# Constants carried by the first key row, an earlier row sum, and gate weights in three blocks, in a two-layer decode kernel

## The chip, the cores and the metric

The kernel runs on one core of one Trainium2 chip. The metric is the device time of one execution in microseconds (us). Repeated runs of one kernel agree within about 0.3%, which is 1.5 us here.

## The reference

One token goes through two identical layers. A layer is attention over the last 4,096 cached positions of 32 heads (head size 192), then a gated MLP; both have a layer norm and a residual.

```python
D, H, DH, F, W = 640, 32, 192, 1536, 4096          # from the inputs' shapes
def attn(x, k_cache, v_cache, wq, wo):
    q = (x @ wq).reshape(heads)                     # 1 x 32 x 192
    p = softmax(einsum("qd,kd->qk", q, k[-W:]) * DH**-0.5)
    return (p @ v[-W:]).reshape(1, H * DH) @ wo
def mlp(x, w_gate, w_up, w_down):
    return (sigmoid(x @ w_gate) * (x @ w_up)) @ w_down
for layer in range(2):                              # the same weights and cache in both
    x = x + attn(layernorm(x), ...)
    x = x + mlp(layernorm(x), ...)
```

Keys and values are 201 MB in bf16 if they are read for both layers. Nothing is reused within a layer: this is a kernel that streams.

## The kernel before

Heads are handled in 16 pairs. A pair's query weights and keys ("a", 28,416 B per partition) and its values and output weights ("b", the same size) fill two of seven slots in the large buffer `big`; the MLP weights use a region behind the slots. A list `seq` fixes the order of all loads, and each load is issued by the sync engine (SP) as soon as the products that still read its destination are done. Three pairs, and the keys of a fourth, are kept for layer 2.

```python
    cst = sb("cst", [P, CE + CE % 2], BF16)       # selectors, masks and x: 241 columns
    big = sb("big", [P, NSLOT * UNIT + ME], BF16, 256)
    # ... cut ...
    MD = {"wg0": (0, 0, 6), "wg2": (6, 6, 12), ...}          # gate weights in two loads of six blocks
    MAFTER = {"d0": ("wg0",), "d1": ("wg1",), "u2": ("wg2",), "u3": ("wg3",), ...}  # who frees whose place
    # ... cut ...
    pg.dma(q_dma(cst[:, 0:CE], cx), "x", wr=[res("cst")], q="adma")   # on the scalar engine's queue
    while seq_pos[0] < 2:                         # first key row, then the first pair load
        assert try_load(seq[seq_pos[0]])
        seq_pos[0] += 1
    # ... cut ...
        def step(p, prev):                        # one pair of layer 1
            ... ; Q(p, 0); QK(p, 0); soft(0, ...); expo(); PVmm(prev, prev % 2); ET(p % 2); PVt(prev % 2)
    # ... cut: the end of the first attention layer ...
            p = NPAIR - 1
            PVmm(p, 1)            # value product of the last pair, waits for its load
            RS(1, 2)              # row sum: ones x (sums of the exponentials), fp32
            PVn(p - 1, 0)         # output product of the pair before
            PVt(1, False)         # transposes of the last pair's result
            PVn(p, 1)             # its output product; then residual, norm, MLP
```

## Time and profile before

| | before |
|---|---|
| time, median of the first 3 runs | 513.43 us |
| span of the profiled run | 511.9 us |
| bytes moved, mean rate | 218.47 MB, 427 GB/s |
| share of the span: TensorE / VectorE / ScalarE busy | 51% / 20% / 17% |
| the last large load lands, the last of two small ones behind it, then the end | 508.97, 509.82, 511.9 us |

From the page of the kernel before: the DMA engines' share in 40 slices (9 is 90% or more), the packets, two queues, the chain that ended last, and the group of the query product (busy time and mean of one, then the idle time before it and who ended most of that).

```profile
DMA  9999999999999999999999999999999999999997
DMA packets 9670, 218.47 MB, mean 427 GB/s; under 512 B 1201, under 2 KB 1586, under 8 KB 4658
q1 hardware_dynamic: 9506, 218.14, 99.3%
q10 hardware_dynamic: 144, 0.06, 0.0%
DMA 64%; PE 22%; DVE 8%; ACT 3%; issue 2%; SPq 1%; DVEq 0%; POOL 0%; ACTq 0%; POOLq 0%
L414 PE MATMUL bank<-sh,big 128*128 128x1 bf16 x465 | 17.1, 166 | 133.2 <-DMA big<-in_uc_dram 130.7
```

The engines that move data are busy in every slice and those that compute are not; the query product spends 130.7 us waiting for loads. Queue q10 is the constants' own: 128 rows and 16 completion packets.

From the timeline of the kernel before, the start (start, length, engine, line, operation, and in brackets the idle time before it with what ended it):

```profile
0.78 0.37 ACTq L217 DMA_DIRECT2D cst<-in_cx_dram  x1
15.41 0.17 DVE L364 TENSOR_SCALAR sc<-cst 128x2 f32<-128x2 bf16 x1 [13.29 <-DMA cst<-in_cx_dram]
...
25.37 0.22 DVE L469 TENSOR_SCALAR sc<-sc 128x2 f32<-128x2 f32 x1
...
28.02 0.56 PE L414 MATMUL bank<-sh,big 128*128 128x1 bf16 x15 [2.83 <-DMA big<-in_uc_dram]
```

The first pair's chain starts when the constants come, at 15.41, ends at 25.6, and TensorE then waits for the next load until 28.02.

And the end of the first attention layer:

```profile
270.59 0.81 PE L494 MATMUL o<-big,et_sb 128*2 128x384 bf16 x8 [0.69 <-DMA big<-in_uc_dram]
271.32 0.59 PE L475 MATMUL bank<-sc 128*128 128x2 f32 x2
...
271.82 0.54 PE L529 MATMUL bank<-sh,big 128*128 128x1 bf16 x15
...
272.45 0.30 PE L515 MATMUL bank<-cst,o_sb 128*128 128x1 bf16 x6
...
275.16 0.96 PE L684 MATMUL scores<-sh,big 128*128 128x1 bf16 x30 [0.60 <-DVE sc L380]
275.75 0.80 SPq L217 DMA_DIRECT2D big<-in_wd_dram  x2
```

Row sum, another pair's output product and only then the transposes stand between the last value product and the MLP; the first down-weight loads are issued at 275.75, when the products of the first three gate blocks are done.

### The profile page before, as it was taken

The page shows a single profiled execution, that of the slowest core. Times are in us where ns is not written, and L with a number is a line of the kernel's source. Part 1 is how long each engine was busy: PE and PEld are TensorE (multiplying, and loading weights), DVE is VectorE, ACT ScalarE, POOL GpSimd, SP SyncE. Part 2 cuts the span into 40 slices and gives each one's busy share as a digit, 9 for nine tenths or more (in the row PEclk, how much of TensorE's full clock was granted, in tenths as well). Part 3 has the DMA queues.
Part 4 walks back from the last instruction along what each step waited for, and adds up shares of the span by engine and source line. Part 5 has one row for each costly group of instructions (what it writes and reads, how often), then busy time and mean ns, then how long its engine had stood idle before and what let it go on. Part 6 is the DMA issues. An engine that isn't in the chain of part 4 may idle for free.

```text
span 511.9 us, 8586 instructions
## 1 busy us (share of the span) xinstructions
PE 260.5 (51%) x3716; PEld 137.7 (27%) x3716; DVE 102.1 (20%) x386; ACT 85.5 (17%) x173; POOL 4.2 (1%) x31
## 2 busy tenths in 40 slices
PE   0463455345533364436566767775725345533666
PEld 0221222122212131223234434432312122212335
DVE  0221221112210221012121333231201112210312
ACT  1110111011101111011121023221211011101221
POOL 0010000000000000000000000000000000000000
PEclk9999765655766755666575568675665655766755
DMA  9999999999999999999999999999999999999997
GB/s 422 435 423 426 419 431 424 431 435 431 453 431 431 436 435 426 431 435 426 424 416 421 414 441 431 434 430 434 439 435 444 435 431 422 436 431 417 429 428 296
DMA packets 9670, 218.47 MB, mean 427 GB/s; under 512 B 1201, under 2 KB 1586, under 8 KB 4658
## 3 DMA queue, kind: packets, MB, share of 16 engines
q1 hardware_dynamic: 9506, 218.14, 99.3%
q8 instruction: 13, 0.21, 0.1%
q10 hardware_dynamic: 144, 0.06, 0.0%
q14 instruction: 7, 0.06, 0.0%
HBM read 218.20 MB, written 0.00 MB: 426 GB/s over the span
## 4 chain that ended last, share of the span: by engine, by line
DMA 64%; PE 22%; DVE 8%; ACT 3%; issue 2%; SPq 1%; DVEq 0%; POOL 0%; ACTq 0%; POOLq 0%
DMA big<-in_uc_dram 54%; PE scores L432 8%; DMA big<-in_wd_dram 6%; PE o L494 6%; DMA big<-in_wu_dram 4%; DVE sc L442 3%; PE bank L448 2%; ACT e_sb L458 2%; PE bank L414 2%; PE bank L529 1%; PE bank L464 1%; ACT diag L445 1%; SPq L217 1%; DVE sc L477 1%; DVE qs L420 1%
## 5 line engine op out<-in xcount | busy, mean ns | idle before, releaser
L432 PE MATMUL scores<-big,qs 128*32 128x512 bf16 x744 | 81.2, 602 | 10.3 <-DVE qs L420 9.5
L414 PE MATMUL bank<-sh,big 128*128 128x1 bf16 x465 | 17.1, 166 | 133.2 <-DMA big<-in_uc_dram 130.7
L494 PE MATMUL o<-big,et_sb 128*2 128x384 bf16 x1024 | 75.1, 460 | 8.0 <-DMA big<-in_uc_dram 3.8
L445 ACT ACTIVATE diag<-cst,sc 128x128 f32<-128x128 bf16 x32 | 12.8, 401 | 306.1 <-DVE sc L442 298.0
L442 DVE TENSOR_REDUCE sc<-scores 128x1 f32<-128x1024 f32 x31 | 37.9, 1224 | 76.9 <-PE scores L432 76.9
L414 PEld LDWEIGHTS bank<-sh,big 128*128 128x128 bf16 x465 | 14.7, 103 | 136.3 <-DMA big<-in_uc_dram 113.6
L448 PE MATMUL bank<-diag,sc 128*128 128x128 f32 x64 | 22.7, 452 | 46.4 <-ACT diag L445 46.4
L458 ACT ACTIVATE e_sb<-scores,sc 128x1024 bf16<-128x1024 f32 x31 | 37.3, 1205 | 42.2 <-DVE sc L453 39.9
L420 DVE TENSOR_TENSOR qs<-bank,cst 128x96 bf16<-128x96 f32 x30 | 7.7, 258 | 161.9 <-PE bank L414 161.9
L494 PEld LDWEIGHTS o<-big,et_sb 128*2 128x2 bf16 x1024 | 27.5, 106 | 43.2 <-issue 28.2
L432 PEld LDWEIGHTS scores<-big,qs 128*32 128x32 bf16 x744 | 23.9, 130 | 42.9 <-issue 29.7
L448 PEld LDWEIGHTS bank<-diag,sc 128*128 128x128 f32 x64 | 14.2, 277 | 72.2 <-ACT diag L445 69.8
L501 ACT CAST o_sb<-o 128x384 bf16<-128x384 f32 x64 | 29.6, 475 | 21.5 <-PE o L494 21.3
L529 PE MATMUL bank<-sh,big 128*128 128x1 bf16 x480 | 17.1, 165 | 15.0 <-DVE sh L518 15.0
L468 DVE CAST et_sb<-bank 128x64 bf16<-128x64 f32 x32 | 7.2, 225 | 70.0 <-PE bank L464 70.0
L529 PEld LDWEIGHTS bank<-sh,big 128*128 128x128 bf16 x480 | 14.5, 99 | 17.5 <-DVE sh L518 12.3
L449 DVE TENSOR_REDUCE sc<-bank 128x2 f32<-128x128 f32 x32 | 9.3, 292 | 43.6 <-PE bank L448 43.6
L464 PE MATMUL bank<-cst,e_sb 128*128 128x8 bf16 x256 | 11.7, 169 | 8.0 <-ACT e_sb L458 7.9
L464 PEld LDWEIGHTS bank<-cst,e_sb 128*128 128x128 bf16 x256 | 8.9, 101 | 23.7 <-issue 17.1
L475 PE MATMUL o<-sc 128*128 128x2 f32 x62 | 14.0, 295 | 0.6 <-ACT o_sb L501 0.6
L475 PEld LDWEIGHTS o<-sc 128*128 128x128 f32 x62 | 12.1, 243 | 2.1 <-ACT o_sb L501 1.3
L477 DVE RECIPROCAL sc<-o 64x1 f32<-64x1 f32 x62 | 10.2, 164 | 9.3 <-PE o L475 7.6
(81 smaller groups left out, 111.0 us busy)
## 6 DMA issues: line engine op xcount, KB each, us to landing
big<-in_uc_dram SPq DMA_DIRECT2D x20, 7104.0 KB, 22.7
big<-in_uc_dram SPq DMA_DIRECT2D x11, 3552.0 KB, 20.5
big<-in_uc_dram SPq DMA_DIRECT2D x2, 3072.0 KB, 18.0
big<-in_uc_dram SPq DMA_DIRECT2D x8, 480.0 KB, 6.5
big<-in_uc_dram SPq DMA_DIRECT2D x1, 2784.0 KB, 13.3
big<-in_uc_dram SPq DMA_DIRECT2D x1, 2304.0 KB, 10.5
big<-in_uc_dram SPq DMA_DIRECT2D x1, 2048.0 KB, 11.0
big<-in_wg_dram SPq DMA_DIRECT2D x2, 960.0 KB, 16.0
```

The lines of the kernel that those rows point to most:

```text
L414: ins = t.matmul(qe[:, i:i + 1], lhsT=w[:, c * 2 * DH + c0:c * 2 * DH + c0 + P], rhs=xq[:, c:c + 1], start=(c == 0), stop=(c == DC - 1))
L432: ins = t.matmul(sc_x[1 + b][32 * j:32 * j + 32, :], lhsT=qs[:, y, k, :], rhs=slot(sa, WQE + k * W + (4 * b + j) * 512, 512), start=(k == ...
L442: pg.op("dve", lambda v: v.reduce_max(out=mx, in_=sc_x[0][:], axis=AX.X), wr=[res("mx")], ex=sc_x[3:5])
L445: pg.op("act", lambda a: a.mul(out=diag[:], in_=ident, mul=mx), rd=[res("cst"), res("mx")], wr=[res("diag")])
L448: pg.op("pe", lambda t: t.matmul(dmx[:, 0:P], lhsT=ones_f, rhs=diag[:], start=True, stop=True), rd=[res("diag"), res("ones")], ex=[rb[2]])
L458: pg.op("act", lambda a: a.activation(out=e_sb[:], in_=sc_x[0][:], func=ACT.Exp, bias=nbias, scale=srs_c, accum_out=rowsum), rd=[res("nbia ...
L464: ins = t.matmul(qe[:, 0:2 * NB].rearrange("p (r x) -> p r x", r=2)[:, :, 4 * b:4 * b + 4], lhsT=e_sb[:, b * P:(b + 1) * P], rhs=sel, star ...
L475: pg.op("pe", lambda t: t.matmul(sm, lhsT=ones_f, rhs=rs2[z], start=True, stop=True), rd=[res(f"rs2{z}"), res("ones")], wr=[res("rsum")], ...
L477: rb[bk].last["dve"] = pg.op("dve", lambda v, h=h: v.reciprocal(out=Rn[z][64 * h:64 * h + 64], in_=sm[64 * h:64 * h + 64, h:h + 1]), rd=[r ...
L494: ins = t.matmul(o8[h][32 * j:32 * j + 2, 0:2 * DH].rearrange("p (a d) -> p a d", a=2), lhsT=et_sb[:, z, h * NB + 2 * u:h * NB + 2 * u + 2 ...
L501: pg.op("act", lambda a, h=h: a.copy(out=o8_sb[:, :, h * DH:(h + 1) * DH], in_=o8[h][:, 0:2 * DH].rearrange("p (a d) -> p a d", a=2)), wr= ...
L529: ins = t.matmul(yT[:, j:j + 1], lhsT=wo[:, c * D + j * P:c * D + (j + 1) * P], rhs=oTb[z][:, c:c + 1], start=False, stop=(c == 2), skip_g ...
```

## The change

The intent: one small, inefficient load less and an earlier first step; a shorter chain from the last values to the MLP; and a first gate block that doesn't wait for six. The constants are placed behind the first key row, in a gap between the fifth and the sixth slot, and arrive with that row.

```diff
-    cst = sb("cst", [P, CE + CE % 2], BF16)
-    big = sb("big", [P, NSLOT * UNIT + ME], BF16, 256)
-    M0 = NSLOT * UNIT
+    GAP = -(-CE // P) * P
+    big = sb("big", [P, NSLOT * UNIT + GAP + ME], BF16, 256)
+    M0 = NSLOT * UNIT + GAP
+    cst = big[:, 5 * UNIT:5 * UNIT + GAP]
-    MD = {"wg0": (0, 0, 6), "wg2": (6, 6, 12), **...}
+    MD = {"wg0": (0, 0, 3), "wg1": (3, 3, 9), "wg3": (9, 9, 12), **...}
     def slot(s, o, n):
-        return big[:, PLACE[s] * UNIT + o:PLACE[s] * UNIT + o + n]
+        o += PLACE[s] * UNIT + (GAP if PLACE[s] > 4 else 0)
+        return big[:, o:o + n]
+            ext = CE if it[1:] == (0, 0) else 0          # the first key row alone
-            pg.dma(q_dma(slot(s, o0, UNIT - o0), a_in(it[2], o0)), ...)
+            pg.dma(q_dma(slot(s, o0, UNIT + ext - o0), a_in(it[2], o0, UNIT + ext)), ...)
-    pg.dma(q_dma(cst[:, 0:CE], cx), "x", wr=[res("cst")], q="adma")
             p = NPAIR - 1
+            RS(1, 2)
             PVmm(p, 1)
-            RS(1, 2)
+            PVt(1, False)
             PVn(p - 1, 0)
-            PVt(1, False)
             PVn(p, 1)
# cut: two asserts, the kernel's argument cx, the empty queue "adma", the host layout
```

More of the change, by code (lines that the diff above doesn't have):

```diff
@@ L109, in decode_kernel @@
 @with_exitstack
-def decode_kernel(ctx: ExitStack, nc, cx: bass.AP, uc: bass.AP,
+def decode_kernel(ctx: ExitStack, nc, uc: bass.AP,
                   wg_d: bass.AP, wu_d: bass.AP, wd_d: bass.AP, wl_d: bass.AP, out: bass.AP):
@@ L186, in decode_kernel @@
           "d0": (0, 0, 3), "d1": (3, 3, 6), "u2": (6, 7, 10), "u3": (9, 10, 12), "d2": (11, 6, 9), "d3": (14, 9, 11), "d4": (16, 11, 12)}
-    MD = {"wg0": (0, 0, 6), "wg2": (6, 6, 12), **{k: v for k, v in MW.items() if k[0] != "w"}}
+    MD = {"wg0": (0, 0, 3), "wg1": (3, 3, 9), "wg3": (9, 9, 12), **{k: v for k, v in MW.items() if k[0] != "w"}}
     MAFTER = {"d0": ("wg0",), "d1": ("wg1",), "u2": ("wg2",), "u3": ("wg3",), "d2": ("wg3", "u0"), "d3": ("u1",), "d4": ("u1",)}
@@ L263, in try_load @@
             first = min(ss, key=PLACE.get)
-            assert abs(PLACE[ss[0]] - PLACE[ss[1]]) == 1 and first == ss[p % 2]
+            assert abs(PLACE[ss[0]] - PLACE[ss[1]]) == 1 and first == ss[p % 2] and PLACE[first] != 4
             pg.dma(q_dma(slot(first, 0, 2 * UNIT), uc[p]), f"c{l}{p % 2}", wr=[rslot[x] for x in ss])
@@ L271, in try_load @@
             o0 = WQE if it[1:] == (1, 3) else 0
-            pg.dma(q_dma(slot(s, o0, UNIT - o0), a_in(it[2], o0)), f"c{it[1]}{it[2] % 2}" if it[1:] in ((0, 15), (1, 4), (1, 5), (1, 6), (1, 13)) else f"a{it[1]}_{it[2]}", wr=[rslot[s]])
+            ext = CE if it[1:] == (0, 0) else 0
+            assert not ext or PLACE[s] == 4
+            pg.dma(q_dma(slot(s, o0, UNIT + ext - o0), a_in(it[2], o0, UNIT + ext)), f"c{it[1]}{it[2] % 2}" if it[1:] in ((0, 15), (1, 4), (1, 5), (1, 6), (1, 13)) else f"a{it[1]}_{it[2]}", wr=[rslot[s]] + ([res("cst")] if ext else []))
         elif k == "b":
@@ L870, in decode_kernel @@
     emit("dma", nc.sync, 1, NFIRST, known_sp)
-    emit("adma", nc.scalar)
     with nc.Block() as block:
@@ L941, in _layout @@
     wl = np.ascontiguousarray(wdn[:, (FC - 2) * D:].reshape(P, 2, 2, D // 2).transpose(0, 2, 1, 3).reshape(P, 2 * D))
-    return dict(cx=cx, uc=uc, wg=blk(wg), wu=blk(wu), wd=wdn, wl=wl)
+    uc[0][:, UNIT:UNIT + CE] = cx
+    return dict(uc=uc, wg=blk(wg), wu=blk(wu), wd=wdn, wl=wl)
 def kernel(**inputs):
```

## The prediction

> **What bounds the kernel now.** The DMA engines, from the first microsecond to the last three. The page gives 218.47 MB at a mean of 427 GB/s and DMA slices of 9 everywhere but the last (7); PE is busy 51%, and idles 133 us in front of the query product, nearly all released by a load. The chain of waits is 64% DMA. The trace's packet records say it more sharply: counting packets open at each moment, all 16 engines are occupied between about 2 and 508 us (under 0.3 us idle per engine there), and the main queue's packets sum to 508.2 us per engine of a span of 511.9. The rest is about 1.0 us before the first packet and 2.9 us after the last load (timeline: it lands at 508.97, then twenty matmuls, copies, the store). So only the engines' work per byte, the start and the tail can move the time.
>
> **What the change removes, adds, moves.**
> 1. Constants. The separate load (60.2 KB, 482 B a row, on the scalar engine's queue) costs 0.224 us per engine (about 27 ns a row). The Trainium skill, "DMA: Bandwidth & Descriptors", "Issuing engines are not separate DMA queues", says that all issuing queues share the 16 engines and interleave; the trace agrees: these packets lie one by one between the main queue's. Rows of 28,416 and 56,832 B take 1,053 and 2,098 ns, 36.8 ns per KB, so 482 B more is an estimated 18 ns, 0.14 us per engine over 8 rows. Saved: 0.08 us.
> 2. Earlier compute. The constants landed near 15.05 us and are first used at 15.41; the first key row's packets were done near 10.2. So the first norm, query, scores and softmax should start near 10.6, almost 5 us earlier. But that chain ends at 25.6 and waits for the second load until 28.0; the wait only grows. On the critical path: 0.
> 3. Gate weights. Two loads of 7,680 B rows become rows of 3,840, 7,680, 3,840 B: by measured packets (291 and 149 ns, 9 ns for the semaphore) an estimated 0.065 us more per engine. The first blocks did not wait for their load before, but for the layer norm (275.16). The first down-weight load is released earlier, the second perhaps 1 us later (it now waits for nine gate blocks, near 276.3); the engines have up weights queued until about 280, so they don't run dry.
> 4. Row sums and transposes early. At the end of the first attention layer PE did the row sum (0.59 us) and the other pair's output product (0.54) between the last value product and the transposes (272.45). Now the transposes follow the copy of the result at 271.93: layer norm and MLP come 0.3 to 0.5 us earlier, and release loads into a queue that isn't empty. Worth 0.
>
> Net: about 0. The tail is untouched.
>
> **Predicted time: 513.35 us, 512.5 to 514.1 (8 in 10).** Chances: faster by over 2% 0.01, within 2% 0.98, slower by over 2% 0.01.
>
> **What would show it.** No second queue among the DMA queues; first-row packets about 18 ns longer; constants' first use near 10.6; the second load still lands near 28 and its query product still waits for it; first gate product near 274.8; DMA share near 1.0 from 256 to 300 us; last load within 0.3 us of 508.97.
>
> **What would make it wrong.** An odd row of 28,898 B cut into many short descriptors (the start tens of us longer); engines running dry near 280 us because the second down block comes late; a different start without the second queue; or instruction fetches shifting when the last engine ends (some tenths).

## The result and the profile after

| | before | after |
|---|---|---|
| median of 6 runs each, same rounds | 513.26 us | 513.30 us |
| lowest and highest | 512.94, 513.54 | 512.95, 513.97 |
| ratio | | 1.0001 (95%: 0.9989 to 1.0014) |
| span of the profiled run | 511.9 us | 511.5 us |
| constants first used | 15.41 us | 11.31 us |

A ratio is the mean time of one kernel's runs over that of the other's runs of the same rounds, so it is not quite the ratio of the medians quoted. The kernels take the same time: the interval is -0.6 to +0.7 us.

The page after, the lines that answer to those of before:

```profile
DMA  9999999999999999999999999999999999999996
DMA packets 9670, 218.47 MB, mean 427 GB/s; under 512 B 1073, under 2 KB 1458, under 8 KB 4658
q1 hardware_dynamic: 9650, 218.20, 99.3%
DMA 63%; PE 22%; DVE 8%; ACT 3%; issue 2%; SPq 1%; DVEq 0%; POOL 0%; ACTq 0%; POOLq 0%
L417 PE MATMUL bank<-sh,big 128*128 128x1 bf16 x465 | 17.1, 166 | 138.0 <-DMA big<-in_uc_dram 135.6
```

The second queue is gone and its 128 short rows with it, and the bytes are the same. The wait of the query product for loads has grown by 4.9 us, from 130.7 to 135.6. Of this, 4.2 us stand before the second pair's query product (2.83 before, 7.00 after): that is where the earlier start went. The timeline after shows it:

```profile
11.31 0.17 DVE L367 TENSOR_SCALAR sc<-big 128x2 f32<-128x2 bf16 x1 [9.20 <-DMA big<-in_uc_dram]
...
21.27 0.22 DVE L472 TENSOR_SCALAR sc<-sc 128x2 f32<-128x2 f32 x1
...
28.10 0.56 PE L417 MATMUL bank<-sh,big 128*128 128x1 bf16 x15 [7.00 <-DMA big<-in_uc_dram]
```

The first pair is done at 21.5 instead of 25.6, and the second pair starts at 28.10 instead of 28.02, because its load lands when it landed before. At the end of the first attention layer:

```profile
268.23 2.73 PE L497 MATMUL o<-big,et_sb 128*2 128x384 bf16 x32 [0.69 <-DMA big<-in_uc_dram]
...
271.55 0.32 PE L518 MATMUL bank<-big,o_sb 128*128 128x1 bf16 x6 [0.58 <-ACT o_sb L504]
271.73 1.19 PE L532 MATMUL bank<-sh,big 128*128 128x1 bf16 x30
...
274.12 0.54 PE L687 MATMUL scores<-sh,big 128*128 128x1 bf16 x15 [0.35 <-DVE sc L377]
...
274.69 2.03 SPq L219 DMA_DIRECT2D big<-in_wd_dram  x2
```

From the end of the last value product to the first gate product it is 3.16 us (270.96 to 274.12) where it was 3.76 (271.40 to 275.16). So the constants and the end of the attention layer did, in the trace, what they were meant to do, and the time did not move. What the gate blocks have to do with the 0.60 us is told with the single parts.

### A count of the engines' work

The packet records of the trace give the bytes and the duration of each packet. By size, the medians are nearly a straight line: 9 ns for a completion packet, 55 for 1,280 B, 149 for 3,840, 291 for 7,680, 573 for 15,360, 1,053 for 28,416, 1,072 for 28,898, 2,098 for 56,832; that is about 8 ns a packet and 36.8 ns per KB (1,000 B). I use these for a balance sheet of every run: the packets of each size times the median duration of that size, with the instruction fetches, summed and divided by 16 engines, is the engines' work. The span less that work is lost time, and I place the losses in stretches of 10 us. Lost time has two parts: engines that stand idle (counted from the packets open at each moment), and packets that take longer than the median of their size. This is arithmetic on the trace, not a view of it.

```
run          span    work   lost at the start   lost elsewhere (stretches with over 0.12 us)      lost from 500 us on
before      511.89  507.31        1.78           60-70: 0.49                                          3.33
after       511.54  507.30        1.85           none                                                 3.65
```

The work differs by 0.01 us. The losses shown add up to 1.0 and 1.3 us more than span less work, because other stretches come out negative (0.5 to 0.6 us from 270 to 300 us, where more than 16 packets are open at a time). But for half a microsecond once in the run of before, where the engines stood for 0.01 us only and the packets of one load took longer, only the start and the tail are lost in either kernel.

### The profile page after: what moved, and what is told of

Same layout as the page of the kernel before. It is cut to its first block, busy times and chain, and to the rows that moved or that the text cites. A ratio compares the mean times of both kernels' runs of the same rounds, so it can differ in the third digit from the quotient of the medians.

```text
span 511.5 us, 8586 instructions
## 1 busy us (share of the span) xinstructions
PE 258.4 (51%) x3716; PEld 136.8 (27%) x3716; DVE 102.2 (20%) x386; ACT 85.1 (17%) x173; POOL 4.2 (1%) x31
## 4 chain that ended last, share of the span: by engine, by line
DMA 63%; PE 22%; DVE 8%; ACT 3%; issue 2%; SPq 1%; DVEq 0%; POOL 0%; ACTq 0%; POOLq 0%
DMA big<-in_uc_dram 54%; PE scores L435 8%; DMA big<-in_wd_dram 6%; PE o L497 5%; DMA big<-in_wu_dram 4%; DVE sc L445 3%; PE bank L451 2%; ACT e_sb L461 2%; PE bank L417 2%; PE bank L532 1%; PE bank L467 1%; SPq L219 1%; ACT diag L448 1%; DVE sc L480 1%; DVE qs L423 1%
## 5 line engine op out<-in xcount | busy, mean ns | idle before, releaser
L417 PE MATMUL bank<-sh,big 128*128 128x1 bf16 x465 | 17.1, 166 | 138.0 <-DMA big<-in_uc_dram 135.6
L497 PE MATMUL o<-big,et_sb 128*2 128x384 bf16 x1024 | 73.3, 452 | 7.2 <-DMA big<-in_uc_dram 3.3
L448 ACT ACTIVATE diag<-big,sc 128x128 f32<-128x128 bf16 x32 | 12.9, 402 | 311.9 <-DVE sc L445 304.0
L451 PE MATMUL bank<-diag,sc 128*128 128x128 f32 x64 | 21.5, 430 | 46.6 <-ACT diag L448 46.6
L423 DVE TENSOR_TENSOR qs<-bank,big 128x96 bf16<-128x96 f32 x30 | 7.7, 258 | 166.9 <-PE bank L417 166.9
L452 DVE TENSOR_REDUCE sc<-bank 128x2 f32<-128x128 f32 x32 | 9.3, 291 | 42.4 <-PE bank L451 42.4
L467 PE MATMUL bank<-big,e_sb 128*128 128x8 bf16 x256 | 11.7, 169 | 8.6 <-ACT e_sb L461 8.5
L467 PEld LDWEIGHTS bank<-big,e_sb 128*128 128x128 bf16 x256 | 8.9, 101 | 24.3 <-issue 17.7
L480 DVE RECIPROCAL sc<-o 64x1 f32<-64x1 f32 x62 | 10.2, 165 | 10.7 <-PE o L478 8.9
```

The costliest lines, as they stand in the source:

```text
L417: ins = t.matmul(qe[:, i:i + 1], lhsT=w[:, c * 2 * DH + c0:c * 2 * DH + c0 + P], rhs=xq[:, c:c + 1], start=(c == 0), stop=(c == DC - 1))
L448: pg.op("act", lambda a: a.mul(out=diag[:], in_=ident, mul=mx), rd=[res("cst"), res("mx")], wr=[res("diag")])
L451: pg.op("pe", lambda t: t.matmul(dmx[:, 0:P], lhsT=ones_f, rhs=diag[:], start=True, stop=True), rd=[res("diag"), res("ones")], ex=[rb[2]])
L467: ins = t.matmul(qe[:, 0:2 * NB].rearrange("p (r x) -> p r x", r=2)[:, :, 4 * b:4 * b + 4], lhsT=e_sb[:, b * P:(b + 1) * P], rhs=sel, star ...
L480: rb[bk].last["dve"] = pg.op("dve", lambda v, h=h: v.reciprocal(out=Rn[z][64 * h:64 * h + 64], in_=sm[64 * h:64 * h + 64, h:h + 1]), rd=[r ...
L497: ins = t.matmul(o8[h][32 * j:32 * j + 2, 0:2 * DH].rearrange("p (a d) -> p a d", a=2), lhsT=et_sb[:, z, h * NB + 2 * u:h * NB + 2 * u + 2 ...
```

## The experiments

The theory (the prediction's): the DMA engines never stand idle between the first microseconds and the tail, so only their work, the start and the tail set the time, and the three parts of the change touch none of these by more than 0.1 us. Rival A: the parts have real effects, of opposite sign, that cancel. Rival B: the compute chain, 22% TensorE in the chain of waits, bounds the kernel, and the gain was lost there.

### One part at a time

Each kernel has one part of the diff above alone: the constants (`p_const`), the order at the end of the first attention layer (`p_sums`), the gate weights' blocks (`p_gate`).

> The kernel before with the first part alone (constants at the end of the first key row). My theory (the DMA engines are never idle, so only their work, the start and the tail count): 513.2 us, within 0.3 us of before; one DMA queue, first use of the constants about 4 us earlier than 15.41, the second load still lands near 28. Rival A (the parts have real effects of opposite sign that cancel in the whole change): this part alone gains over 1 us.

> The kernel before with the second part alone (row sum before the last value product, transposes before the other pair's output product). My theory: within 0.3 us of before; the first gate product about 0.5 us earlier against the landing of the last values, the DMA engines busy as before. Rival A: over 1 us faster or slower.

> The kernel before with the third part alone (gate weights in 3, 6 and 3 blocks). My theory: within 0.3 us of before, 0.065 us more engine time. Rival A: this part loses over 1 us and hides the gain of the constants.

| part alone | median | before, same rounds | ratio (95%) | span | engines' work |
|---|---|---|---|---|---|
| constants | 513.26 us | 513.62 us | 0.9991 (0.9977 to 1.0005) | 512.0 | 507.24 us |
| sums and transposes | 513.12 us | 513.62 us | 0.9991 (0.9977 to 1.0004) | 511.9 | 507.31 us |
| gate blocks | 513.48 us | 513.62 us | 1.0002 (0.9989 to 1.0016) | 511.7 | 507.38 us |

The work of the engines answers to the costing: 0.07 us less with the constants (predicted 0.08), 0.07 more with the gate blocks (predicted 0.065), none from the order. The times can't resolve that. What they do say is that each part is worth between -1.2 and +0.8 us, so of rival A only a cancellation smaller than about 1 us is left, and the work leaves no place for it. These lines of the pages show the two kernels' packets; the constants save the second queue, the gate blocks add 144 packets (128 rows and 16 completions) to the 9,506 of before.

```profile
q1 hardware_dynamic: 9506, 218.20, 99.2%
q8 instruction: 13, 0.21, 0.1%
```

```profile
q1 hardware_dynamic: 9650, 218.14, 99.2%
q8 instruction: 13, 0.21, 0.1%
q10 hardware_dynamic: 144, 0.06, 0.0%
```

The first is the page of the constants alone, the second that of the gate blocks alone.

The first gate product shows that two parts need each other. In before its load of six blocks landed at 275.11 us, just before the product began at 275.16. With the order alone (first line) the product waits for this load, and comes 3.68 us after the last value product (271.03), hardly sooner than the 3.76 of before (counted from the landing of the last values 4.61 us and 4.62, so the expected 0.5 us was missed). With three blocks in the first load alone (second line) it waits for the norm and comes after 3.50 us (from 271.16). Both together give the 3.16.

```profile
274.71 0.96 PE L684 MATMUL scores<-sh,big 128*128 128x1 bf16 x30 [1.10 <-DMA big<-in_wg_dram]
```

```profile
274.66 0.54 PE L684 MATMUL scores<-sh,big 128*128 128x1 bf16 x15 [0.35 <-DVE sc L374]
```

### More bytes

One load more in the changed kernel:

```diff
     busy.add(2)
     prefetch()
+    pg.dma(q_dma(mreg(0, 12 * FW), wg_d), "xtra", wr=rc[0:12])   # 1.97 MB into a free region, not used
```

> The changed kernel with one more load of 1.97 MB (the gate weights, 15,360 B a row, into a region that is free then, issued behind the second pair load, at about 1.6 us; its data is not used and the result is right). My theory: rows of 15,360 B take 573 ns, 8 of them on each engine 4.6 us, and all of it is added to the time: 517.9 us (517.5 to 518.3). Rival B (the chain of waits, with its 22% of TensorE and 8% of VectorE, bounds the kernel and the loads have slack): less than 1.5 us is added.

517.84 us against 513.62: ratio 1.0083 (1.0069 to 1.0097), which is +4.3 us (3.5 to 5.0) for an expected 4.6. The work is 511.91 us, 4.61 more than after, and the losses are those of before and after (1.88 at the start, 3.50 in the tail, 0.20 once between). The page of this run:

```profile
DMA packets 9814, 220.44 MB, mean 427 GB/s; under 512 B 1089, under 2 KB 1474, under 8 KB 4674
q1 hardware_dynamic: 9794, 220.17, 99.3%
```

Loads have no slack: extra engine work is paid in full, although SP and the compute engines had tens of microseconds of idle time where it was put. Rival B expected under 1.5 us.

### More compute

One product more per softmax, again in the changed kernel:

```diff
             pg.op("pe", lambda t: t.matmul(dmx[:, 0:P], lhsT=ones_f, rhs=diag[:], start=True, stop=True), ...)
+            pg.op("pe", lambda t: t.matmul(dmx[:, 0:P], lhsT=ones_f, rhs=diag[:], start=True, stop=True), ...)
```

> The changed kernel with the fp32 product that spreads the row maxima over the partitions done twice, in all 32 softmaxes (0.4 to 0.8 us each in the chain, some 20 us of TensorE in all; result right). My theory: within 0.5 us of the changed kernel, since every step still ends before the loads issued earlier run out (smallest margin in the pair loop 4.6 us). Rival B: 10 us or more is added.

513.73 us against 513.31 of before in the same rounds: 1.001 (0.9993 to 1.0026), -0.4 to +1.3 us. In the run's view of the added line, its products (64 instructions for 32 softmaxes):

```profile
L452 PE MATMUL bank<-diag,sc x64: 275/421/422, 18.4 to 487.2; 128*128 128x128 f32 x64
```

The step behind this product waits for it longer, in after and then in this run (us, times):

```profile
  DVE sc L452: 42.4, 32
```

```profile
  DVE sc L453: 51.2, 32
```

TensorE does 64 more products of 421 ns in the median, right in the chain of every pair. The chain grew by 8.8 us in all (51.2 less 42.4), somewhat less than the 10 us that I had given to rival B, and nothing is lost in the balance sheet (work 507.30, one stretch with 0.14 us). The 22% of TensorE in the chain of waits is therefore not a claim on the time: that view follows the last releaser, and a compute step that releases a buffer early enough is on its path without costing anything. Rival B falls.

### A later start: how much the first step may slip

If an earlier first step is worth nothing, a later one should be worth nothing too, up to a point that the queue sets. Three kernels, all made from before, delay it:

```diff
-    pg.dma(q_dma(cst[:, 0:CE], cx), "x", wr=[res("cst")], q="adma")
+    # late_const: on the load queue, behind the first two loads
+    pg.dma(q_dma(cst[:, 0:CE], cx), "x", wr=[res("cst")])
```

```diff
+    for _ in range(5):                        # s5_before; 8 in s8_before
+        pg.op("dve", lambda v: v.reduce_max(out=mx, in_=o8_ps[:], axis=AX.X), rd=[res("cst"), res("o8z"), res("mx")], wr=[res("mx")])
     pg.op("dve", lambda v: v.tensor_scalar(out=wsel, in0=pm, scalar1=1.0 / 16, ...), rd=[res("cst")], ...)
```

> The kernel before with the constants issued on the load queue behind the second load, so that they land near 28 us instead of 15: the first query, scores and softmax (10.2 us long in the trace of before) start near 28.3. The next buffer is then released near 49.6 instead of 39.1, while the loads already issued last until 45.66: my theory says the engines stand idle for about 5 us there (issue to first packet is 1.0 us in the trace), and only that is lost: 518.5 us (517 to 520). Rival B (the chain counts as it stands): the whole delay of about 12.9 us is lost. Were the early start of compute worth anything in the change, it would show here already at the first microseconds of delay.

> The kernel before with five VectorE maxima over 128x1024 (1.23 us each in the trace, 6.2 us) between the arrival of the constants and the first norm: the changed kernel's 4 us turned round. First step 6 us later; it ends near 31.8 instead of 25.6, so the second step starts 3.9 us late and the third pair load is issued near 43.0, some 1.5 to 2.7 us before the loads ahead of it run out (44.4 in one trace, 45.7 in another), and 0.95 us pass from an issue to the first packet. My theory: 513.4 us, at most 0.4 us lost. Rival B: 6 us, or the 3.9 us of the second step's delay.

> The same with eight maxima, 9.8 us. The third pair load is issued near 46.8, past the end of the queue; packets start 0.95 us later and all engines within 1.5: my theory, now with the terms that the late constants had wrong (queue empty at 44.4 to 45.7, not 45.66 flat; 0.95 to 1.5 us to packets): about 3.0 us lost, 516.4 us (515.5 to 517.2).

A first form of the last two had a race (the maxima read a bank without waiting for the write that clears it) and was not run; the wait was added.

| | first step begins | third pair load issued | median | before, same rounds | ratio (95%) | lost in the trace there |
|---|---|---|---|---|---|---|
| before | 15.41 us | 39.14 us | | | | 0 |
| five maxima | 21.7 | 42.07 | 514.58 us | 513.72 us | 1.0023 (1.0010 to 1.0037) | 0.40 us (40 to 50 us) |
| eight maxima | 25.4 | 46.26 | 518.18 us | 513.72 us | 1.0092 (1.0077 to 1.0108) | 3.99 us (40 to 50 us) |
| constants late | 27.95 | 50.62 | 521.30 us | 513.31 us | 1.0149 (1.0134 to 1.0164) | 8.30 us (40 to 60 us) |

The windows of four runs, the stretch from 44 to 48 us (busy time of PE, PEld, DVE, ACT and POOL with instruction counts, then the granted clock, the DMA engines' share and GB/s): before, five maxima, eight maxima, constants late.

```profile
44.00:48.00 4.00, 1.46 (x27) 0.85 (x31) 0.26 (x1) 0.00 (x0) 0.09 (x1) 1.00 0.82 355
```

```profile
44.00:48.00 4.00, 1.71 (x27) 0.93 (x31) 0.26 (x1) 0.00 (x0) 0.09 (x1) 0.50 0.98 398
```

```profile
44.00:48.00 4.00, 2.98 (x70) 2.06 (x70) 1.07 (x6) 0.48 (x1) 0.09 (x1) 0.93 0.69 213
```

```profile
44.00:48.00 4.00, 2.89 (x30) 1.45 (x34) 1.02 (x4) 1.93 (x4) 0.09 (x1) 1.00 0.00 0
```

A packet counts in the window where it starts, and packets of 56,832 B are 2.1 us long, so a single short window is rough (before shows 0.82 with no idle time by the packet records); but the last line, with no byte in 4 us, leaves no doubt. The direction is as the theory has it: a first step 6 us late costs the time little, one 10 us late costs 4, one 12.5 us late costs 8. Rival B's figures (6 or 3.9, and 12.9) are not met. But all three of my sizes were too small (with five maxima the clock shows 1.2 us, where I expected 0.4 at most), and the terms can be named.

- Constants late: 5 us expected, 8 measured. I had written 49.6 for the issue and 45.66 for the end of the queue. The issue was at 50.62, because one operation took 1.67 us instead of 0.17: it ran beside the only GpSimd copy of the kernel and ended 0.02 us after it (the two lines below; an ordinary run of the same operation is the line at 15.41 us of before). The Trainium skill, "SBUF — State Buffer", "SBUF: two separate sides", says that VectorE in some modes and GpSimd share one pair of ports under an exclusive lock, so the one that comes second waits for the other's whole instruction; this agrees in one instance, 1.5 us for an operation on two columns; in which mode it ran, no trace shows.

```profile
27.82 1.78 POOL L356 COPY big<-big 128x1920 bf16<-128x1920 bf16 x1
27.95 1.67 DVE L364 TENSOR_SCALAR sc<-cst 128x2 f32<-128x2 bf16 x1 [25.82 <-DMA cst<-in_cx_dram]
```

- The end of the queue, 45.66, is that of its slowest engine. In before, the 16 completion packets of that load come at 43.71 to 44.38 us for fifteen engines and at 45.65 for one; in the late kernel all come between 43.81 and 44.37. (An instruction fetch of 16 KB, 0.88 us long, ran at 33.8 us in before and at 43.8 in the late kernel; it may be what delayed one engine: after, five and eight maxima, with the fetch at 33.4 to 39.7 us, have one late engine too, at 45.3 to 45.5. But its 0.88 us explain only half, so the cause is left open.) The mean engine is dry at 44.0, 1.6 us before the figure I used.
- From an issue to the first packet 0.95 us pass (50.62 to 51.57), and the sixteenth engine starts at 52.16, 1.54 us after the issue; with eight maxima it is 0.96 and 1.75 us, and the mean engine starts 1.1 to 1.2 us after the issue in both.
- The first packets after a pause are longer: 2.3 to 3.6 us in these two runs, where the median of 56,832 B is 2.10. I had no term for that, and why it is so no run shows.

With these terms the losses close. With eight maxima the engines stood from 44.13 to 47.38 in the mean, 3.25 us, and longer packets make up the other 0.74 of the 3.99; with the constants late they stood from 44.07 to 51.78, 7.71 us, and longer packets are the other 0.6 of the 8.30. With five maxima they stood for only 0.08 us of the 0.40: nearly all of that loss is longer packets, though the load was issued 1.8 us before its first packet. So a load that comes late costs something before the engines stand. By the ratio the three lose 1.2, 4.7 and 7.7 us; the losses in the trace (0.40, 3.99, 8.30) lie within the interval for the last two and 0.1 us below it for five maxima; that profiled run of five also lost 0.23 us near 280, for which I have no cause.

### A later MLP: how much the end of the attention layer may slip

```diff
             PVn(p, 1)
+            for _ in range(4):               # d4_before, d4_after; 2 in d2_before
+                pg.op("dve", lambda v: v.reduce_max(out=mx, in_=e_sb[:], axis=AX.X), rd=[res("e"), res("mx")], wr=[res("mx")])
```

> The kernel before with two maxima (2.5 us of VectorE, of which 1.0 us hides behind the last output product, so about 1.4 us in the chain) before the first MLP. The chain's margin there was 3.06 us, 1.5 to 2.1 of it usable: my theory: nothing lost, 513.3 us within 0.4. If 1.4 us or more is lost, the chain and not the queue bounds this stretch.

> The kernel before with four extra VectorE maxima over 128x1024 (an estimated 1.2 us each, 4.9 us in all) between the last output product of the first attention layer and the residual sum. By the trace, the first down-weight load is issued 3.06 us before the queue would run dry there, 2 us of it usable if 1.0 us passes from issue to first packet: my theory says about 3 us of the 4.9 are lost, engines idle near 280 us: 516.3 us (515 to 517.5). Rival A or B: 0 (loads elsewhere make up for it) or all 4.9.

> The same four maxima in the changed kernel. There the first down-weight load is issued 3.73 us before the queue runs dry, and the gate products that release it come about 1 us earlier; my theory: about 2.4 us lost, 515.7 us, some 0.6 us (0.3 to 1.0) less than the same delay in the kernel before. If the two agree, the change bought no margin either.

| | first down-weight load issued | median | before, same rounds | ratio (95%) | lost in the trace, 270 to 300 us |
|---|---|---|---|---|---|
| before | 275.75 us | | | | none over 0.12 |
| after | 274.69 | | | | none over 0.12 |
| before, two maxima | 277.19 | 514.47 us | 513.72 us | 1.0017 (1.0003 to 1.0030) | 0.95 us |
| before, four maxima | 279.33 | 516.19 us | 513.31 us | 1.0054 (1.0042 to 1.0066) | 2.92 us |
| after, four maxima | 278.69 | 515.97 us | 513.31 us | 1.0048 (1.0034 to 1.0063) | 2.55 us |

The windows from 277 to 281 us of before, of before with two and with four maxima, and of after with four:

```profile
277.00:281.00 4.00, 2.47 (x67) 2.31 (x67) 0.40 (x2) 0.73 (x3) 0.00 (x0) 0.50 1.02 416
```

```profile
277.00:281.00 4.00, 2.96 (x89) 2.79 (x85) 0.40 (x2) 0.73 (x3) 0.00 (x0) 0.50 0.96 352
```

```profile
277.00:281.00 4.00, 2.83 (x72) 2.77 (x73) 1.31 (x9) 0.03 (x1) 0.00 (x0) 0.50 0.48 150
```

```profile
277.00:281.00 4.00, 3.46 (x96) 3.41 (x97) 0.68 (x9) 0.61 (x3) 0.00 (x0) 0.50 0.62 199
```

Here the engines do run dry with four maxima, from 278 to 280 us, and the time lost is mostly the time they stand: 2.8 us by the ratio, 2.9 by the balance, of which they stood 2.33, of the 3.9 us by which the chain was really delayed (residual at 277.61 instead of 273.74). Of the two places that I delayed, this has less to spare. I delayed no other, and in the second layer of before a load is issued only 2.5 us ahead of its first packet (364.36 and 366.89).

Two maxima move the issue by 1.44 us and already cost 0.95 in the trace and 0.9 (0.2 to 1.5) by the ratio, where I expected nothing. The engines stood for only 0.28 us of it; the rest is packets that took longer. My "1.5 to 2.1 us usable" was counted to 278.81, by bytes landed, and again had no term for longer packets. With four maxima the first engine was dry at 277.6, the mean one at 278.2 and the last at 279.5, and the mean engine worked again 1.1 us after the issue. To standing engines the margin of before is then an estimated 1.4 us (278.2 less 1.1 less 275.75); to the first loss it is smaller, since two maxima used up 1.44 us and lost 0.9.

The same delay costs the changed kernel 2.55 us in the trace against 2.92: the change bought some margin at this place. The times do not resolve it (1.0048 and 1.0054 with overlapping intervals), so I call it shown by two traces only. The table leaves out stretches under 0.12 us; by the time that the engines stood (2.33 and 1.68 us) the difference is 0.65 us, the 0.6 expected.

### An extra load in narrow rows: a faulty experiment

> The same extra bytes as in the wide extra load, but as 24 loads with rows of 640 B. A packet costs about 8 ns and 36.8 ns per KB by the trace's sizes (1,280 B 55 ns, 28,416 B 1,053 ns), a semaphore 9 ns: 31.5 ns a row, 24 x (8 x 31.5 + 9) ns = 6.3 us per engine: 519.6 us, 1.7 us over the wide one. This is the price per packet with which I costed the gate weights' split (0.065 us).

```diff
+    for i in range(24):                       # rows of 640 B, two loads to one block of the region
+        pg.dma(q_dma(mreg(i * 320, 320), wg_d[:, i * 320:(i + 1) * 320]), "xtra", wr=rc[i * 320 // FW:-(-(i + 1) * 320 // FW)])
```

546.33 us against 513.72, ratio 1.0643: 33 us where 6.3 were expected. The edit was at fault, not the price. The kernel's bookkeeping works by blocks of 1,280 B; two of my loads share one, so every second load waited on SP until the one before it had landed, and from 46 to 73 us the engines were busy only 27% of the time. From the timeline of SP and the window of that stretch in this run:

```profile
1.67 71.92 SPq L219 DMA_DIRECT2D big<-in_wg_dram  x24
```

```profile
46.00:73.00 27.00, 8.03 (x102) 3.83 (x98) 5.14 (x16) 2.54 (x5) 0.00 (x0) 0.56 0.27 67
```

The comparison of wide and narrow rows by time is thus lost. The packet records still hold the price: 640 B took 32 ns in the median (31.5 expected), and the run's work is 513.66 us, 1.75 over the wide one's 511.91 (1.7 expected). And the run is, unasked, the largest test of the theory: 25.1 us of the balance's losses lie between 40 and 80 us (the engines stood for 23.0 of them), and about 33 us were added for 6.4 of work.

No run points to a version that beats both kernels beyond what the clock resolves: 507.3 of the 511.9 us are work on bytes that both kernels move, about 1.8 the start and about 3 the tail.

## Why the prediction was right

- "The DMA engines, from the first microsecond to the last three": right, and the core of it. The balance finds 507.31 us of work in 511.9; more work was paid in full, more compute was free, and apart from added work only experiments that left the queue empty, or nearly so, cost time.
- Constants, saved 0.08 us: right; 0.07 in the work of the part alone. The rows took 1,072 ns instead of 1,053, 19 more for the 18 predicted.
- "The first norm ... should start near 10.6": it was 11.31. The mis-sized term is the end of the first key row, which I put near 10.2 by its earliest completions; after the change the last engine's came at 11.00 and VectorE started 0.3 us later. Its worth, 0, was right: the wait for the second load grew (TensorE's from 2.83 to 7.00 us before the second query product), and even a start 6 us later than before cost about 1 us.
- Gate weights, 0.065 us: right, 0.07. "The first blocks did not wait for their load before, but for the layer norm": wrong. Their load landed at 275.11 and they began at 275.16; the gate blocks alone saved 0.26 us there (3.50 instead of 3.76), and without them the earlier norm would have been lost in the wait for the load (3.68). That it was worth 0 all the same is right for the reason given, a queue that isn't empty. "Up weights queued until about 280" holds for the slowest engine (their last load landed at 280.09 in before); the mean engine is dry near 278.2 (seen with four maxima), so the margin was 1.8 us smaller than I had written. The conclusion held, since the first down-weight loads were issued at 274.69 and 276.39, still early enough, and not thanks to the size of that margin. The second load, put near 276.3, came 0.24 us later than before, not 1.
- Row sums and transposes, 0.3 to 0.5 us earlier: right for the residual sum, which comes 2.00 us after the last value product (272.96) instead of 2.34; the gate product comes 0.6 us earlier, but only together with the gate blocks. Worth 0: right here, since the engines were not dry.
- "Last load within 0.3 us of 508.97": 508.62 in the profiled run, 0.35 off. This is not the last load, as I wrote: two small ones behind it land until 509.82 in before and 509.39 in after, so 2.1 us and not 2.9 follow the last load. The engines' work is the same; the loss of 0.49 us between 60 and 70 us, seen in the profiled run of before and not in that of after, is of this size. Six runs each put the kernels level.

## What to carry to other kernels

When the DMA engines are busy from end to end, price a change in engine work first (bytes, packets, completions), then ask of every earlier or later wait one question: does the next load still get issued before the first engine runs dry, less what an issue needs? That was 1.1 to 1.2 us here until the mean engine worked, and 1.8 us were still too few to keep the first packets from growing longer (five maxima). If yes on both sides of the change, it is worth nothing, whatever its share of the chain of waits. And count what is lost to the mean engine's last packet, not to a later end: that overstated the margin by 1.6 us at the start (45.66 for 44.0) and by 0.6 before the MLP (278.81 for 278.2).

## What the Trainium skill lacked or had wrong

- "DMA: Bandwidth & Descriptors", "Where 436 GB/s comes from": it says that for loads from HBM the HBM side binds near 358 GB/s per core. (Its own table has 425 for one load of 16 MB, with a note that the neighbouring core was idle; the sentence lacks this condition.) Here one core, in a program of one core, loaded 218 MB at a mean of 427 GB/s over the whole execution, and packets of 56,832 B ran at 27.1 GB/s per engine, 433 GB/s for 16.
- The same page, "Why small descriptors are slow (HBM only)": it gives about 3 cycles per packet and 32 bytes of descriptor metadata. The packets here fit about 8 ns each plus 36.8 ns per 1,000 B, from 640 B (32 ns) to 56,832 B (2,098 ns). The page has no such line for loads issued from SP.
- The same page, "Latency and other measured facts", gives about 600 ns to the first byte for such loads, and does not say from when. Here the first packet's record begins 0.95 to 1.0 us after the issue begins and 0.62 us after the issue's own 0.33 us end (late constants: 50.62, 50.95, 51.57), so it agrees if counted from there. It lacks that the last of 16 engines starts 1.5 to 1.8 us after the issue begins, and that the first packets after a pause take longer (2.3 to 3.6 us for 2.10).
- No page says by how much the engines of one load can end apart, which decides how early the next load must be issued: 43.7 to 44.4 us for fifteen and 45.65 for one.
